# Late values on even steps to the end, masked whole-partition copies of turned P, memory copied before rows, early stores behind the weights, all priority tables re-tuned

## The chip, the cores and the metric

One core of a Trainium2 chip (trn2) runs the whole program; the other cores are idle. The metric is the device time of one launch in microseconds (us), lower is better. The kernel was already tuned: TensorE was busy 97% of the time. Before the change it took a median of 1673.75 us (1672.41 to 1676.7, 4 runs beside the changed kernel). In what follows PE is TensorE (matmuls; PEld its weight loads), DVE is VectorE, ACT is ScalarE, POOL is GpSimd, SP is SyncE; SBUF and PSUM are the two memories in which the program places its tiles; the outputs of the matmuls are in PSUM, in tiles that the program calls banks.

## The reference

Two layers of the same form, each a memory-augmented attention and a dense block with ReLU. The sequence (2048 tokens of width 512) is cut into 64 segments of 32 tokens. In front of each segment stand 8 memory tokens, so a step works on L = 40 tokens with 32 heads of width 128. The memory for the next segment is the first 8 rows of this segment's output: a recurrence over 64 steps.

```python
for s in range(n_seg):                       # 64 segments
    h = concat([mem, x[:, s*32:(s+1)*32]])   # 8 + 32 rows
    q, k, v = h @ Wq, h @ Wk, h @ Wv         # 32 heads x 128
    p = softmax(where(mask, q @ k.T * scale, -1e9))
    o = (p @ v) @ Wo
    mem = o[:, :8]                           # the next step needs this
    outs.append(o[:, 8:])
# x = x + attn(ln(x)); x = x + relu(ln(x) @ w1) @ w2; twice, same weights
```

The kernel runs the two layers interleaved: layer 2 follows 4 steps behind layer 1, so there are 68 steps, and steps 4 to 63 work on 80 columns (40 of each layer). I call these the steady steps. Two of them make a pair, since the dense block and the loading of new rows come once in two steps.

## The kernel before

Every operation is put into a plan with a priority; a small list scheduler in the program then decides which engine runs what and in which order. The priorities come from tuned tables (`PLACE`, `AHEAD`, `RULE`).

```python
def rank(c):     # among the ops that could start now; `stay` favours the tile width now set
    return (c[1].prio - (stay if PE in c[1].cost and c[1].tile in (tile, EITHER) else 0.0), c[1].seq)
```

The stages of a step on PE: Q and K of all heads ("Q/K"), scores, turn of P (a transpose by the identity), attend (PT times V), project (times Wo). The 32 heads of a step go through in five units of 8 or 4 heads. Between the scores and the turn of a unit lies its softmax chain: DVE adds the mask, takes the row maximum and subtracts it, ACT takes the exponentials, DVE takes the sum and its reciprocal, and a product gives P. The result of an attend is copied ("evicted") from PSUM to OT, which the project reads. `COL64` operations use the array in tiles of 64 columns, others in 128; in before's trace a matmul after a change of width starts later. The weights are issued in one fixed order, since each of the DMAs writes the plan's key `"issue"`:

```python
for c, p0, n in (("v",0,1), ("v",1,1), ("v",2,2), ...qk 0, qk 2, o 0, o 2...):
    ...
    plan.op(POOL, 0.75, dma, w=["issue", ("issued", c, p0), ...], lag=1.5)
    plan.op(QUEUE, LOAD * n, land, r=[("issued", c, p0)], w=[("W", c, p0 + i)..., "queue"])
```

After the turn, P is copied from PSUM to SBUF as PT, each of the two heads of a pair into its half of the partitions; the other half stays zero:

```python
for b in range(2):
    def keep(eng, b=b):
        R = slice(64 * b, 64 * b + 64)
        copy_on(eng, PT[R, a_lo:a_hi, 0:2 * nx, b, :], tp[R, A].rearrange(...))
    copy_op(n, keep, r=[tp, PT, "zero PT"], w=[(PT, b)])
```

After the project its bank is read twice: the memory goes to HT, where the next Q/K reads it, and the rows go to OX for the dense block. In the plan the memory copy `ev` and the row copy `rows` are free of each other; in the trace the two reads of the bank follow each other, and here ACT's row copy comes first (DVE's memory copy waits for it for 190.7 us in all, see the page below):

```python
    plan.op(DVE, 0.15, ev, r=[wo], w=[("HTm", i)])          # memory -> HT
    ...
    copy_op(NC4 * SEG * len(aa), rows, r=[wo, "zero ox"], w=[ox])   # rows -> OX
```

"Late values" are V of layer 1's rows for later steps (the row half that does not need the memory). They have much time, so they serve as filling for PE. Groups 5 to 15 are spread over steps near `4 * g - LEAD`, that is until step 43:

```python
for g in range(1, NG):
    plan.mark(*((0, f"g{g}") if g <= EARLY else (4 * g - LEAD - 1, "r")))    # EARLY, LEAD = 4, 8
    prepare_group(g)
```

Of the kernel before, what the change touches and what calls it, by code (L numbers as in the profile page):

```python
# [8 lines left out]
BF = mybir.dt.bfloat16  # L9
# [20 lines left out]
RULE = (0.0474, 165.9433, 849.1155, 931199.0135)  # L30
PERIOD = 35.7447
PLACE = {
    ("attend.mmu0.0", 0): -216.486, ("attend.mmu0.0", 1): 347.606, ("attend.mmu1.0", 0): 191.045,
    ("attend.mmu1.0", 1): -37.14, ("attend.mmu2.0", 0): -46.771, ("attend.mmu2.0", 1): -87.486,
    ("attend.mmu3.0", 0): -34.251, ("attend.mmu3.0", 1): 122.032, ("attend.mmu4.0", 0): 152.031,
    ("attend.mmu4.0", 1): -58.366, ("dense_layer.mm.0", 1): 553.611, ("dense_layer.mm.1", 1): 518.055,
    ("dense_layer.mm.2", 1): 535.954, ("dense_layer.mm.3", 1): 582.949, ("dense_layer.mm.4", 1): 549.423,
    ("dense_layer.mm.5", 1): -563.126, ("finish_pair.turn.0", 1): -571.909, ("g0", 0): 141.998, ("g1", 0): 105.737,
    ("g2", 0): -45.394, ("g3", 0): -40.982, ("g4", 0): 105.238, ("layernorm.turn.0", 1): 118.646,
    ("layernorm.turn.1", 1): 41.01, ("layernorm.turnr.0", 1): -256.199, ("prepare.turns.0", 0): 734.35,  # L40
    ("project.mm.0", 0): 563.031, ("project.mm.0", 1): 33.894, ("project.mm.1", 0): 542.081,
    ("project.mm.1", 1): 183.384, ("project.mm.2", 0): -30.084, ("project.mm.2", 1): 230.376,
    ("project.mm.3", 0): 464.585, ("project.mm.3", 1): 57.605, ("project.mm.4", 0): 4.192,
    ("project.mm.4", 1): -119.585, ("queries_keys.mmu0.0", 0): 15.305, ("queries_keys.mmu0.0", 1): -52.287,
    ("queries_keys.mmu0.1", 0): -466.697, ("queries_keys.mmu0.1", 1): -132.577, ("queries_keys.mmu0.2", 0): 87.033,
    ("queries_keys.mmu0.2", 1): 5.362, ("queries_keys.mmu0.3", 0): -44.757, ("queries_keys.mmu0.3", 1): 81.556,
    ("queries_keys.mmu1.0", 0): 54.963, ("queries_keys.mmu1.0", 1): -50.581, ("queries_keys.mmu1.1", 0): -37.389,
    ("queries_keys.mmu1.1", 1): -11.489, ("queries_keys.mmu1.2", 0): 124.613, ("queries_keys.mmu1.2", 1): 46.342,
    ("queries_keys.mmu1.3", 0): -10.32, ("queries_keys.mmu1.3", 1): -54.319, ("queries_keys.mmu2.0", 0): 131.134,
    ("queries_keys.mmu2.0", 1): 110.056, ("queries_keys.mmu2.1", 0): 188.57, ("queries_keys.mmu2.1", 1): 86.427,  # L50
    ("queries_keys.mmu2.2", 0): 136.518, ("queries_keys.mmu2.2", 1): 105.68, ("queries_keys.mmu2.3", 0): -9.099,
    ("queries_keys.mmu2.3", 1): 98.244, ("queries_keys.mmu3.0", 0): 163.016, ("queries_keys.mmu3.0", 1): 110.95,
    ("queries_keys.mmu3.1", 0): 14.03, ("queries_keys.mmu3.1", 1): 192.637, ("queries_keys.mmu4.0", 0): 339.974,
    ("queries_keys.mmu4.0", 1): 257.046, ("queries_keys.mmu4.1", 0): 340.503, ("queries_keys.mmu4.1", 1): 207.593,
    ("scores.mmu0.0", 0): 149.552, ("scores.mmu0.0", 1): 125.149, ("scores.mmu1.0", 0): 35.849,
    ("scores.mmu1.0", 1): -5.001, ("scores.mmu2.0", 0): 16.784, ("scores.mmu2.0", 1): -51.948,
    ("scores.mmu3.0", 0): 244.506, ("scores.mmu3.0", 1): 56.245, ("scores.mmu4.0", 0): -45.271,
    ("scores.mmu4.0", 1): 447.766, ("scores.turnu0.0", 0): 194.57, ("scores.turnu0.0", 1): 55.105,
    ("scores.turnu1.0", 0): -573.079, ("scores.turnu1.0", 1): 162.901, ("scores.turnu2.0", 0): 146.776,
    ("scores.turnu2.0", 1): -13.477, ("scores.turnu3.0", 0): -142.712, ("scores.turnu3.0", 1): -557.814,  # L60
    ("scores.turnu4.0", 0): -32.301, ("scores.turnu4.0", 1): -558.239, ("values.mm.0", 0): 140.097,
    ("values.mm.0", 1): -46.466, ("values.mm.1", 0): 100.105, ("values.mm.1", 1): 168.241,
    ("values.mm.2", 0): 161.203, ("values.mm.2", 1): 105.472, ("values.mm.3", 0): 200.739,
    ("values.mm.3", 1): -82.814, ("values.mmv0.0", 0): 542.558, ("values.mmv1.0", 1): 574.532,
    ("values.mmv2.0", 0): 480.688, ("values.mmv3.0", 1): 180.687, ("values_narrow.mm.0", 0): 119.158,
    ("values_narrow.mm.0", 1): 313.862, ("values_narrow.mm.1", 0): 19.413, ("values_narrow.mm.1", 1): 340.719,
}
AHEAD = {
    "*late_values.cp": 68.026, "*late_values.put": 167.527, "*layernorm.aggr": -134.458, "*layernorm.eps": -12.177,
    "*layernorm.keep": 157.484, "*layernorm.norm": 235.062, "*layernorm.power": 306.224,  # L70
    "*layernorm.stats": -113.935, "*prepare_group.load": -308.983, "*prepare_group.put": 11.73,
    "*values.ev": 65.226, "attend.ev": -242.579, "dense_layer.relu": -6.21, "dense_layer.relu_last": 178.105,
    "finish_pair.add": -242.042, "finish_pair.add0": -173.051, "finish_pair.add1": -93.035,
    "finish_pair.store": 188.752, "finish_pair.widen": 52.721, "late_values.cp": 212.468, "late_values.put": 18.071,
    "layernorm.aggr": -157.294, "layernorm.eps": 204.671, "layernorm.keep": 168.993, "layernorm.norm": -34.524,
    "layernorm.power": 58.2, "layernorm.stats": 74.815, "load_dense.dma1": 13.513, "load_dense.dma2": 72.207,
    "load_group.get": 70.644, "load_group.load": -212.738, "load_weights.dma": 57.711, "load_weights.hold": 170.204,
    "load_weights.land": -60.531, "make_ident": 215.071, "make_mask": -24.221, "place_values.dma": 32.686,
    "prep_x.cp": -77.977, "prepare.get_memory": -28.532, "prepare.get_x": 90.295, "prepare.keep": 326.132,
    "prepare.place": -93.726, "prepare.zero": 217.012, "prepare.zero_banks": 114.762,  # L80
    "prepare.zero_columns": 19.064, "prepare_group.load": 158.644, "prepare_group.put": 153.519,
    "project.ev": 154.095, "project.first": 306.336, "project.rows": -72.228, "queries_keys.ev": 233.354,
    "scores.block": 179.729, "scores.exp": 6.954, "scores.keep": 236.149, "scores.mul": 385.392,
    "scores.recip": -258.069, "scores.sub": 5.745, "scores.top": -100.433, "scores.total": 132.559,
    "values.ev": 91.194, "values_narrow.ev": -145.426,
}

LOAD = 2.75

EARLY, LEAD = 4, 8  # L90
# [10 lines left out]
def t_dve(n, rate=1):  # L101
    return 0.065 + 1.042e-3 * n / rate

# [51 lines left out]
class Plan:  # L155
# [55 lines left out]
    def order(self):  # L211
# [31 lines left out]
        while left:  # L243
# [32 lines left out]
            for b in o.banks:  # L276
                for i in range(6):
                    if i != e:
                        b.held[i] = max(b.held[i], o.end + LAT[e][i])
# [17 lines left out]
def kernel(  # L297
# [73 lines left out]

    def load_weights():



        for c, p0, n in (("v", 0, 1), ("v", 1, 1), ("v", 2, 2), *((c, p0, 2) for cc, p0 in (("qk", 0), ("qk", 2), ("o", 0), ("o", 2)) for c in cc)):
            def dma(c=c, p0=p0, n=n):
                if c == "o":
                    hs = slice(8 * p0, 8 * (p0 + n))
                    nc.gpsimd.dma_start(out=Wo_sb[:, hs, :], in_=A_Wo.rearrange("h e d -> e h d")[:, hs, :])  # L380
                else:
                    cs = slice(p0 * PW, (p0 + n) * PW)
                    nc.gpsimd.dma_start(out=W_s[c][:, :, cs], in_=W_v[c][:, :, cs])

            plan.op(POOL, 0.75, dma, w=["issue", ("issued", c, p0), *(["issued"] if c == "v" else [])], lag=1.5)

            def land():
                pass

            plan.op(QUEUE, LOAD * n, land, r=[("issued", c, p0)], w=[*[("W", c, p0 + i) for i in range(n)], "queue"])  # L390

        def hold():
            nc.sync.dma_start(out=held[:], in_=Wo_sb[0:1, H - 1, 0:16])

        plan.op(SP, 0.78, hold, r=[("W", "o", 2)], w=["loaded"], lag=0.0)

    def load_dense():
# [3 lines left out]
        def dma2():  # L401
            nc.gpsimd.dma_start(out=w2_sb[:, 0:NFC - 1, :],
                                in_=B_w2[0:(NFC - 1) * 128, :].rearrange("(c p) d -> p c d", p=128))
            nc.gpsimd.dma_start(out=w2_sb[0:F_LAST, NFC - 1, :], in_=B_w2[(NFC - 1) * 128:Dff, :])
# [53 lines left out]
    def prepare():  # L458
# [6 lines left out]
        def zero_banks():  # L465
            for t in b_work.tiles:
                nc.vector.memset(t[:], 0.0)
# [648 lines left out]
```

## Time and profile before

| what | number |
|---|---|
| median time | 1673.75 us |
| span of the profiled run | 1673.3 us, clock 0.995 |
| PE busy | 1621.0 us (97%) |
| end of step 0, of step 3, of step 63, of step 67 | 56.72, 115.77, 1585.81, 1659.12 us |

The step ends are the starts of the last project matmul of that step, from the trace. The page of the kernel before, its first part (busy time, share, count), slices of 1/40 of the span with PE's busy tenths and granted clock, and the chain of waits (shares by line):

```profile
PE 1621.0 (97%) x39689; PEld 1388.0 (83%) x39689; DVE 1049.8 (63%) x3065; ACT 1093.0 (65%) x2759; POOL 127.9 (8%) x337
...
PE   6899999999999999999999999999999999999997
...
PEclk9999999999999999999999999999999999999998
...
PE 84%; DVE 8%; issue 3%; ACT 3%; DMA 2%; POOL 0%; POOLq 0%; DVEq 0%; ACTq 0%
```

So PE bounds the kernel, and what counts is what stands between its matmuls. Busy time does not tell that, because matmuls overlap: one of 80 columns counts as busy for 202 ns, but the next one starts 36 ns after it. I therefore took the starts of neighbouring matmuls from the trace: each form has a median start-to-start time (80 columns 36 ns, 40 columns 25 ns, two 64-wide tiles of 512 columns together 216 ns), whose sum is the work ("floor"); a start after a change of tile width comes later; what is left is waiting.

| before | span | work | width changes | their price | waits |
|---|---|---|---|---|---|
| to the end of step 3 | 115.8 us | 77.3 | 39 | 3.7 | 22.8 (+ 11.9 before the first matmul) |
| steps 4 to 63 | 1470.0 | 1389.9 | 462 | 43.4 | 36.8 |
| steps 64 to 67 | 73.3 | 66.0 | 30 | 2.8 | 4.5 |

At the start the last weight decides. The chain of waits of before, in order of time (start us, us, what):

```profile
16.27 6.02 PE fill L780 x32
...
24.97 29.75 DMA Wo_sb<-in_A_Wo_dram
54.77 2.17 PE st L996 x64
```

The second half of Wo is issued last and lands at 54.8 us. PE is not idle until then, though: Wq and Wk land before it (25.0 to 43.2 us), and the windows of the timeline (start:end, length, busy time with count of PE, PEld, DVE, ACT, POOL, then PE's clock, DMA share, GB/s) show PE busy for 17.7 of the 20 us from 20 to 40. The third line below is a stretch without late values, where PE loses 3% more:

```profile
20.00:40.00 20.00, 17.69 (x310) 10.98 (x308) 6.36 (x21) 10.14 (x23) 5.70 (x16) 1.00 1.03 379
...
300.00:600.00 300.00, 299.14 (x7210) 257.26 (x7210) 193.80 (x548) 206.29 (x509) 22.31 (x62) 1.00 0.11 28
...
1200.00:1500.00 300.00, 291.29 (x7126) 252.94 (x7123) 192.25 (x540) 197.13 (x485) 17.06 (x42) 1.00 0.08 20
```

The copies that the change touches, from the groups of instructions by form (busy us, mean ns; then idle time in front and its releaser). HT, the memory copy, waits for ACT's row copy:

```profile
L721 ACT CAST PT<-work 64x320 bf16<-64x320 f32 x330 | 139.5, 423 | 14.4 <-DVE PT L723 9.6 <-PE work L516 2.7
...
L723 DVE CAST PT<-work 64x160 bf16<-64x160 f32 x188 | 60.3, 321 | 25.6 <-PE work L516 23.5
...
L1012 DVE CAST HT<-st 128x64 bf16<-128x64 f32 x60 | 13.5, 225 | 190.7 <-ACT OX L721 190.7
```

### The profile page before, as it was taken

The page shows a single profiled execution, that of the slowest core. Times are in us where ns is not written, and L with a number is a line of the kernel's source. Part 1 is how long each engine was busy: PE and PEld are TensorE (multiplying, and loading weights), DVE is VectorE, ACT ScalarE, POOL GpSimd, SP SyncE. Part 2 cuts the span into 40 slices and gives each one's busy share as a digit, 9 for nine tenths or more (in the row PEclk, how much of TensorE's full clock was granted, in tenths as well). Part 3 has the DMA queues.
Part 4 walks back from the last instruction along what each step waited for, and adds up shares of the span by engine and source line. Part 5 has one row for each costly group of instructions (what it writes and reads, how often), then busy time and mean ns, then how long its engine had stood idle before and what let it go on. Part 6 is the DMA issues. An engine that isn't in the chain of part 4 may idle for free.

```text
span 1673.3 us, 87959 instructions
## 1 busy us (share of the span) xinstructions
PE 1621.0 (97%) x39689; PEld 1388.0 (83%) x39689; DVE 1049.8 (63%) x3065; ACT 1093.0 (65%) x2759; POOL 127.9 (8%) x337
## 2 busy tenths in 40 slices
PE   6899999999999999999999999999999999999997
PEld 3688888888888888888888888888888888888886
DVE  5466656665665675566667566566656656665664
ACT  3566766766676676666667666666666666666664
POOL 4110000000000010100000000000000000000000
PEclk9999999999999999999999999999999999999998
DMA  9811010111101111000110100000000000000000
GB/s 348 265 45 32 24 29 26 29 32 29 27 24 32 28 30 31 28 24 27 28 29 24 31 25 24 26 26 22 17 25 18 24 20 16 18 19 16 16 6 6
DMA packets 34473, 64.70 MB, mean 39 GB/s; under 512 B 7242, under 2 KB 17874, under 8 KB 34098
## 3 DMA queue, kind: packets, MB, share of 16 engines
q1 hardware_dynamic: 27858, 39.38, 8.4%
q0 software_dynamic: 4624, 18.19, 3.0%
q8 instruction: 311, 5.10, 1.3%
q10 hardware_dynamic: 1616, 1.52, 0.3%
q14 instruction: 64, 0.52, 0.1%
HBM read 33.89 MB, written 12.45 MB: 28 GB/s over the span
## 4 chain that ended last, share of the span: by engine, by line
PE 84%; DVE 8%; issue 3%; ACT 3%; DMA 2%; POOL 0%; POOLq 0%; DVEq 0%; ACTq 0%
PE work L860 32%; PE st L996 18%; PE fill L780 16%; PE fill L516 10%; PE work L969 3%; PE work L889 3%; PE work L516 3%; DMA Wo_sb<-in_A_Wo_dram 2%; DVE P L930 1%; DVE mx L904 1%; DVE es L907 1%; DVE sm L914 1%; DVE es L900 1%; ACT es L911 1%; DVE kT L723 1%
## 5 line engine op out<-in xcount | busy, mean ns | idle before, releaser
L860 PE MATMUL work<-HT,Wk_sb 128*128 128x80 bf16 (+1 forms) x8704 | 357.5, 200 | 1.6 <-issue 1.0
L860 PE MATMUL work<-HT,Wq_sb 128*128 128x80 bf16 (+1 forms) x8704 | 345.6, 199 | 3.9 <-issue 3.9
L996 PE MATMUL st<-OT,Wo_sb 128*128 128x80 bf16 (+1 forms) x8704 | 347.9, 199 | 1.2 <-DMA Wo_sb<-in_A_Wo_dram 0.9
L860 PEld LDWEIGHTS <-Wk_sb 128*128 128x128 bf16 x8704 | 322.3, 99 | 29.0 <-issue 17.2
L996 PEld LDWEIGHTS <-Wo_sb 128*128 128x128 bf16 x8704 | 322.7, 100 | 12.0 <-DMA Wo_sb<-in_A_Wo_dram 1.0
L860 PEld LDWEIGHTS <-Wq_sb 128*128 128x128 bf16 x8704 | 317.4, 99 | 6.3 <-issue 3.9
L721 ACT CAST kT<-work 128x320 bf16<-128x320 f32 (+1 forms) x481 | 197.1, 410 | 130.3 <-PE work L860 98.6
L780 PE MATMUL fill<-Wv_sb,HT 128*64 128x512 bf16 x2048 | 261.3, 382 | 0.0
L900 DVE TENSOR_TENSOR es<-work,maskb 128x320 f32<-128x320 f32 (+2 forms) x340 | 137.1, 405 | 185.9 <-PE work L889 180.0
L721 ACT CAST qT<-work 128x320 bf16<-128x320 f32 (+1 forms) x509 | 208.6, 412 | 57.1 <-PE work L860 16.8
L721 ACT CAST OT<-work 128x320 bf16<-128x320 f32 (+1 forms) x400 | 157.6, 421 | 119.0 <-PE work L969 115.5
L721 ACT CAST vw<-fill 128x512 bf16<-128x512 f32 x263 | 153.7, 585 | 95.0 <-PE fill L780 87.2
L721 ACT CAST PT<-work 64x320 bf16<-64x320 f32 (+2 forms) x454 | 172.8, 382 | 20.6 <-DVE PT L723 9.6
L914 DVE TENSOR_REDUCE sm<-es 128x8 f32<-128x320 f32 (+2 forms) x340 | 134.8, 398 | 41.4 <-ACT es L911 37.7
L911 ACT ACTIVATE es<-es 128x320 f32<-128x320 f32 (+2 forms) x340 | 138.6, 410 | 23.9 <-DVE es L907 22.6
L780 PEld LDWEIGHTS <-HT 128*64 128x64 bf16 x2048 | 97.0, 109 | 64.7
L1012 DVE CAST HT<-st 128x64 bf16<-128x64 f32 (+1 forms) x67 | 14.8, 222 | 207.9 <-ACT OX L721 207.9
L930 DVE TENSOR_TENSOR P<-es,sm 128x320 bf16<-128x320 f32 (+2 forms) x336 | 141.7, 424 | 5.2
L907 DVE TENSOR_TENSOR es<-es,mx 128x320 f32<-128x320 f32 (+2 forms) x340 | 140.6, 416 | 4.6
L904 DVE TENSOR_REDUCE mx<-es 128x8 f32<-128x320 f32 (+2 forms) x340 | 135.2, 400 | 5.6
L889 PEld LDWEIGHTS <-qT 128*40 128x40 bf16 x4096 | 91.5, 98 | 49.5 <-ACT qT L721 3.3
L969 PE MATMUL work<-PT,V 128*128 128x80 bf16 (+1 forms) x1188 | 108.9, 202 | 1.4 <-ACT PT L721 0.5
(89 smaller groups left out, 1761.7 us busy)
## 6 DMA issues: line engine op xcount, KB each, us to landing
V<-vw SPq DMA_DIRECT2D x252, 48.0 KB
V<-vh SPq DMA_DIRECT2D x126, 64.0 KB
vh<-vg SPq DMA_DIRECT2D x22, 256.0 KB
Wq_sb<-in_A_Wq_dram POOLq DMA_DIRECT2D x2, 2048.0 KB, 18.1
Wk_sb<-in_A_Wk_dram POOLq DMA_DIRECT2D x2, 2048.0 KB, 23.0
Wo_sb<-in_A_Wo_dram POOLq DMA_DIRECT2D x2, 2048.0 KB, 27.8
Wv_sb<-in_A_Wv_dram POOLq DMA_DIRECT2D x2, 1024.0 KB, 6.4
Wv_sb<-in_A_Wv_dram POOLq DMA_DIRECT2D x1, 2048.0 KB, 10.8
```

The lines of the kernel that those rows point to most:

```text
L516: nc.tensor.matmul(out_[u:v, :], lhsT=lhsT[:, u:v], rhs=rhs, start=start, stop=stop, tile_position=(0, u))
L721: nc.scalar.copy(out=out_, in_=in_)
L780: nc.tensor.matmul(vp[64 * b:64 * b + 64, :], lhsT=cols[:, c4, :], rhs=Wv_sb[:, c4, n * 512:(n + 1) * 512], start=(c4 == 0), stop=(c4 == N ...
L860: nc.tensor.matmul(qp[:, hi * 2 * L:hi * 2 * L + n], lhsT=W_sb[:, c4, h * Dh:(h + 1) * Dh], rhs=HT[:, c4, c0:c1], start=(c4 == 0), stop=(c ...
L900: nc.vector.tensor_tensor(out=flat(es[:, A]), in0=flat(sp[:, A]), op=ALU.add, in1=maskb[:, a_lo:a_hi, :].unsqueeze(2).to_broadcast([128, n ...
L904: nc.vector.tensor_reduce(out=mx[:, As], in_=es3(), axis=AX.X, op=ALU.max)
L907: nc.vector.tensor_tensor(out=es3(), in0=es3(), op=ALU.subtract, in1=mx[:, As].unsqueeze(2).to_broadcast([128, ns * na, L]))
L911: nc.scalar.activation(out=es[:, A], in_=es[:, A], func=ACTF.Exp, scale=SCALE)
L914: nc.vector.tensor_reduce(out=sm[:, As], in_=es3(), axis=AX.X, op=ALU.add)
L930: (nc.gpsimd if eng == POOL else nc.vector).tensor_tensor(out=o, in0=flat(es[:, A]), op=ALU.mult, in1=sm[:, As].rearrange("p (a s) -> p a ...
L969: nc.tensor.matmul(o[u:u + cols, :, a, :], lhsT=V[:, p, e0 + u:e0 + u + cols], rhs=PT[:, a, 2 * i + h2, :, :], start=True, stop=True, tile ...
L996: nc.tensor.matmul(wo[:, 2 * W * c4 + c0:2 * W * c4 + c1], lhsT=Wo_sb[:, h, c4 * 128:(c4 + 1) * 128], rhs=OT[:, h, c0:c1], start=(h == 0 a ...
```

## The change

Its intent: keep filling for PE up to the end (late values on even steps until step 57), take the memory out of the project's bank before the rows, so that Q/K starts sooner, replace half-partition copies of PT by whole-partition copies with a 0/1 mask as the scale, store the early values behind the weights, and re-tune all tables. The diff, cut to its core (the tables `RULE`, `PERIOD`, `PLACE`, `AHEAD` are new throughout; helpers for buffers, layer norm and zeroing are left out):

```diff
-LOAD = 2.75
-EARLY, LEAD = 4, 8
+LOAD, LOAD_O = 2.55, 2.9
+EARLY, LAST, PACE = 5, 57, 1.3
...
+    def bulk(eng, t, fn, name, size, r=(), w=(), rate=LOAD):
+        plan.op(eng, t, fn, r=r, w=[("issued", *name)], lag=1.5)
+        plan.op(QUEUE, rate * size, land, r=[("issued", *name)], w=[*w, "queue"])
...
-            plan.op(POOL, 0.75, dma, w=["issue", ("issued", c, p0), ...], lag=1.5)
+            bulk(POOL if (c, p0) != ("v", 0) else SP, 0.78, dma, (c, p0), n, w=[...],
+                 rate=LOAD_O if c == "o" else LOAD)
...
             def keep(eng, b=b):
-                R = slice(64 * b, 64 * b + 64)
-                copy_on(eng, PT[R, a_lo:a_hi, 0:2 * nx, b, :], tp[R, A].rearrange(...))
+                o, i = PT[:, a_lo:a_hi, 0:2 * nx, b, :], tp[:, A].rearrange(...)
+                if eng == ACT:
+                    nc.scalar.activation(out=o, in_=i, func=ACTF.Copy, scale=half[:, b:b + 1])
+                else:
+                    nc.vector.tensor_scalar_mul(out=o, in0=i, scalar1=half[:, b:b + 1])
...
-            plan.op(DVE, 0.15, ev, r=[wo], w=[("HTm", i)])
+            plan.op(DVE, 0.15, ev, r=[wo], w=[("HTm", i), ("taken", k)])
...
-            copy_op(NC4 * SEG * len(aa), rows, r=[wo, "zero ox"], w=[ox])
+            copy_op(NC4 * SEG * len(aa), rows, r=[wo, ("taken", k)], w=[ox])
...
+    for i in range(4 * (NG - 1 - EARLY)):          # 40 late values on even steps up to LAST
+        g, p = EARLY + 1 + i // 4, i % 4
+        k = int(LAST - PACE * (4 * (NG - 1 - EARLY) - 1 - i)) // 2 * 2
+        due.setdefault(k, []).append((g, p))
...
+            late_values(g, late[g], [p], [("att", k - 1)])
```

The key `"issue"` is gone, so the scheduler may reorder the weights.

## The prediction

> **What bounds the kernel now.** TensorE's instruction stream. The page's first part has PE busy 1621.0 of 1673.3 us, ACT and DVE at 65% and 63%; the chain that ended last is 84% PE. I priced the stream by start-to-start times of neighbouring matmuls in the trace (80 columns 36 ns, 40 columns 25 ns, 512 columns 216 ns for two 64-wide tiles together). The 39689 matmuls need 1536 us. Besides: 12 us before the first; 532 changes of tile width (128/64/32 columns), 0.115 us extra each, 61 us; other waits 59 us (about 20 before 100 us, 32 from 100 to 1640, 7 at the end); 5 us of tail. [...]
>
> **What the change moves.** By the order of instructions:
> 1. Matmul work is the same (1535 us), but width changes fall from 532 to 366, mostly 4 and 6 per step instead of 7 and 9. 166 x 0.115 = 19 us, all on the critical path. The main gain.
> 2. Late values. Today they run out near step 43; from 1100 us the timeline shows two waits per pair of steps (0.95 us before the P turn, 0.63 us after the project), 1.9 us per pair against 0.25 earlier. After, fill lasts to step 57, so the 0.95 goes: 10 pairs, roughly -10 us.
> 3. Memory ahead of rows. Today ACT copies rows (0.37 us), then DVE the memory (0.225); where little fills it, Q/K starts 0.93 us after the project's last matmul. Memory first makes that 0.24 + 0.225 + 0.055 = 0.52 us. But the new order has no fill between odd-step projects and the next Q/K, so it is paid at every second step: 0.48 x 30 = 15 us, against some 8 today. After even steps 0.65 us of dense matmuls hides it.
> 4. Masked PT copies: same count and elements; consecutive half-partition DVE copies start 0.33 us apart, whole ones 0.23-0.25 (160 elements). Off the path.
> 5. Start. Today the second Wo half lands last, at 54.8 us, 1507 us of matmuls left. After, Wo goes ahead of the second Wq, the first load goes out 1.5 us earlier, 0.5 MB of stores (at about 350 GB/s) move behind the weights: last weight near 52 us (estimate), but 1511 us left. Net about zero.
> 6. Tail unchanged: a serial dense layer, clock granted at half from 1663 us. [...]
>
> **Sum.** 1673 - 1 (work) - 19 (widths) - 3 (waits: -10 + 7) - 1 (start) = about 1649. Range 1636 to 1662.
>
> **What would show it.** Widths: fewer changes at the same price, steady pair of steps 49.2 -> about 48.4 us. Late values: no 0.95 waits after 1100 us. Memory: DVE's HT copy 0.24 us after the project's last matmul (0.64 today); a wait near 0.5 us after odd steps. Start: step 3's project ending near 115 us (116 today).
>
> **What would make it wrong.** Longer one-width runs leave softmax chains less room: in odd steps a P3 turn follows its scores by 2.7 us of PE time (3.05 the shortest today): a few tenths per pair cost 5-10 us. At the start, the last units' Q/K now wait for the last weights with the softmax chain behind[...].

What the trace shows is a median of 0.10 us and a mean of 0.115 us for a change of width as I read it then (0.094 in the later reading of the median), a granted clock of 0.50 from 1663 us to the end, and a wait of 3.85 us in front of a Q/K matmul at 71.59 us, for which the profile shows no releaser.

## The result and the profile after

The changed kernel took a median of 1670.11 us (1669.17 to 1670.9, 4 runs) against 1673.75 us, a ratio of 0.9976 with a 95% interval of 0.9958 to 0.9993: about 4 us faster, within 2%, and outside the predicted range of 1636 to 1662. A ratio here is the mean time of one kernel's fast runs over that of the other's in the same rounds, so it is not quite the ratio of the quoted medians. The profiled span was 1669.2 us at a clock of 0.992.

The page of after, first part, slices and the chain:

```profile
PE 1605.1 (96%) x40146; PEld 1376.4 (82%) x40206; DVE 1098.7 (66%) x3043; ACT 1051.7 (63%) x2662; POOL 160.0 (10%) x387
...
PE   4899999999999999999999999999999999999997
...
PEclk8999999999999999999999999999999999999999
...
PE 82%; DVE 12%; issue 2%; DMA 2%; ACT 1%; ACTq 0%; POOL 0%; POOLq 0%; DVEq 0%
```

PE has 40146 records but PEld 40206: 60 records of the dense block's second matmul (w2) are missing from this trace. For the split of the steady steps I therefore use the run a_issue below, which has all records, the same steady order of matmuls in kind and count, and nearly the same steady span (1461.55 against 1461.34 us).

| | before | after | difference |
|---|---|---|---|
| first matmul | 11.9 us | 7.8 | |
| end of step 3 | 115.77 | 121.61 | +5.8 |
| steps 4 to 63 | 1470.04 | 1461.34 | -8.7 |
| of it width changes, price | 462, 43.4 | 304, 28.9 | -14.5 |
| of it waits | 36.8 | 42.7 | +5.9 |
| steps 64 to 67 | 73.31 | 73.15 | -0.2 |
| after step 67 | 14.14 | 13.08 | -1.1 |
| span | 1673.3 | 1669.2 | -4.1 |

The start got longer although the first matmul came 4 us earlier. The chain of waits of after, its first lines that matter, and then what PE waited for (in total, times, longest):

```profile
8.89 26.30 DMA Wq_sb<-in_A_Wq_dram
...
35.23 1.78 PE work L906 x48
```

```profile
PE work L906 <- DMA Wq_sb<-in_A_Wq_dram: 11.3, 2, 10.5
PE work L906 <- DVE HT L1061: 11.1, 36, 0.3
PE fill L493 <- DMA ob<-in_A_mem_dram: 7.8, 1, 7.8
PE work L532 <- DVE P L976: 5.9, 12, 0.9
```

PE stood still for 10.5 us, until 35.2 us, for the first half of Wq. POOL's timeline shows why: the first half of Wo and the first half of Wk went out in front of it.

```profile
2.35 1.77 POOL L391 DMA_DIRECT2D Wv_sb<-in_A_Wv_dram  x2
4.09 1.18 POOL L388 DMA_DIRECT2D Wo_sb<-in_A_Wo_dram  x1
...
5.83 0.78 POOL L391 DMA_DIRECT2D Wk_sb<-in_A_Wk_dram  x1
...
8.89 0.83 POOL L391 DMA_DIRECT2D Wq_sb<-in_A_Wq_dram  x1
```

The windows of the timeline show PE busy for 9.0 instead of 17.7 us from 20 to 40, with the granted clock at 0.66 of full. The half clock (0.50) was granted from 26.0 to 39.7 us: from 1.3 us after the end of the last matmul, as the profile models it (24.7 us), until 4.5 us after the next one's start. What sets these two moments is not shown. The windows also show that the loss without late values is gone (294.6 of 300 us busy from 1200 to 1500, 291.3 before), while from 300 to 600 PE is busy for less than before (a_issue, which has all records, has 295.9 us there, so most of that is real).

```profile
20.00:40.00 20.00, 9.02 (x134) 5.83 (x132) 4.47 (x11) 4.54 (x10) 2.88 (x7) 0.66 1.03 371
...
300.00:600.00 300.00, 295.09 (x7313) 253.83 (x7322) 206.68 (x548) 194.37 (x478) 27.72 (x67) 1.00 0.10 27
...
1200.00:1500.00 300.00, 294.58 (x7316) 254.44 (x7325) 205.97 (x548) 193.63 (x478) 26.86 (x65) 1.00 0.09 23
```

The copies, from the groups by form. Masked copies take about 0.1 us longer each (530 against 423 ns on ACT), and HT is now released by PE's project and no longer by ACT's OX:

```profile
L999 ACT ACTIVATE PT<-work,half 128x320 bf16<-128x320 f32 x101 | 52.5, 530 | 8.1 <-DVE PT L1001 7.2
...
L1001 DVE TENSOR_SCALAR PT<-work,half 128x320 bf16<-128x320 f32 x259 | 137.0, 539 | 2.2 <-ACT PT L999 0.3
...
L1061 DVE CAST HT<-st 128x64 bf16<-128x64 f32 x60 | 13.5, 225 | 159.6 <-PE st L1045 159.6
```

Where the waits of the steady steps lie, per pair of steps (steps 14 to 61, from the starts of matmuls; the price of 0.094 us of a width change is taken off):

| wait in front of | before | after | a_half | a_short | a_swap | a_pt |
|---|---|---|---|---|---|---|
| Q/K or OX turn, behind an odd project | 0.24 us | 0.48 | 0.48 | 0.48 | 0.89 | 0.48 |
| Q/K, behind the dense block | - | - | - | - | 0.24 | - |
| turn, behind scores | 0.66 | 0.16 | 0.17 | 0.16 | 0.15 | 0.16 |
| turn, behind attend | 0.18 | 0.32 | 0.57 | 0.24 | 0.32 | 0.32 |
| attend, behind the dense block (w1) | - | 0.27 | 0.34 | - | 0.27 | - |
| turn, behind a part of the project | - | 0.05 | 0.15 | - | 0.06 | 0.28 |

A dash is under 0.04 us. So in 30 pairs the waits behind scores fell by some 15 us, those behind the odd project rose by 7, and new waits at attend and turn cost some 14: together the +6 of the table above.

The order of instructions shows what happened to the filling. In before the late values lie one to a step up to step 43. In after all of them lie at the end of odd steps (1 or 2 each), up to step 55, and nothing at all stands between an odd project and the next Q/K.

### The profile page after: what moved, and what is told of

It reads as the page before. It is cut to its first block, busy times and chain, and to the rows that moved or that the text cites. A ratio compares the mean times of both kernels' runs of the same rounds, so it can differ in the third digit from the quotient of the medians.

```text
span 1669.2 us, 88991 instructions
## 1 busy us (share of the span) xinstructions
PE 1605.1 (96%) x40146; PEld 1376.4 (82%) x40206; DVE 1098.7 (66%) x3043; ACT 1051.7 (63%) x2662; POOL 160.0 (10%) x387
## 4 chain that ended last, share of the span: by engine, by line
PE 82%; DVE 12%; issue 2%; DMA 2%; ACT 1%; ACTq 0%; POOL 0%; POOLq 0%; DVEq 0%
PE work L906 34%; PE st L1045 18%; PE fill L826 14%; PE fill L532 7%; PE work L1018 4%; PE work L935 3%; DVE PT L1001 3%; PE work L532 2%; DVE mx L950 2%; DVE es L953 2%; DMA Wq_sb<-in_A_Wq_dram 2%; DVE es L946 1%; DVE sm L960 1%; DVE OT L764 1%; DVE P L976 1%
## 5 line engine op out<-in xcount | busy, mean ns | idle before, releaser
L906 PE MATMUL work<-HT,Wk_sb 128*128 128x80 bf16 (+1 forms) x8704 | 368.6, 199 | 11.8 <-DVE HT L1061 11.1
L906 PE MATMUL work<-HT,Wq_sb 128*128 128x80 bf16 (+1 forms) x8704 | 362.4, 200 | 11.5 <-DMA Wq_sb<-in_A_Wq_dram 11.3
L906 PEld LDWEIGHTS <-Wk_sb 128*128 128x128 bf16 x8704 | 329.8, 99 | 37.9 <-issue 27.2
L906 PEld LDWEIGHTS <-Wq_sb 128*128 128x128 bf16 x8704 | 325.8, 100 | 25.0 <-issue 13.4
L762 ACT CAST kT<-work 128x320 bf16<-128x320 f32 (+1 forms) x539 | 223.3, 414 | 96.2 <-PE work L906 60.3
L762 ACT CAST vw<-fill 128x512 bf16<-128x512 f32 x233 | 136.5, 586 | 147.2 <-PE fill L826 143.1
L1001 DVE TENSOR_SCALAR PT<-work,half 128x320 bf16<-128x320 f32 (+2 forms) x357 | 172.2, 493 | 18.6 <-PE work L532 13.6
L999 ACT ACTIVATE PT<-work,half 128x160 bf16<-128x160 f32 (+2 forms) x323 | 127.3, 430 | 37.3 <-PE work L532 26.6
L728 DVE TENSOR_TENSOR xg<-xg,fill 128x512 f32<-128x512 f32 (+1 forms) x34 | 23.4, 688 | 166.1 <-PE fill L532 161.5
L976 DVE TENSOR_TENSOR P<-es,sm 128x160 bf16<-128x160 f32 (+1 forms) x304 | 121.0, 409 | 4.1
```

The costliest lines, as they stand in the source:

```text
L762: nc.scalar.copy(out=out_, in_=in_)
L906: nc.tensor.matmul(qp[:, hi * 2 * L:hi * 2 * L + n], lhsT=W_sb[:, c4, h * Dh:(h + 1) * Dh], rhs=HT[:, c4, c0:c1], start=(c4 == 0), stop=(c ...
L976: (nc.gpsimd if eng == POOL else nc.vector).tensor_tensor(out=o, in0=flat(es[:, A]), op=ALU.mult, in1=sm[:, As].rearrange("p (a s) -> p a ...
L1001: nc.vector.tensor_scalar_mul(out=o, in0=i, scalar1=half[:, b:b + 1])
```

## The experiments

My theory after the result had three parts. (1) The start lost 10 us because the weights were reordered. (2) In the steady steps the longer one-width runs leave the softmax chains less room, which makes new waits. (3) Memory first and masked copies move these waits. The rival for (2), my first guess, was that the masked copies themselves, each 0.1 us longer, are the new cost. Sixteen kernels ran besides after; all were correct. Every ratio is against before in the same rounds.

| run | what | median us | ratio (95%) |
|---|---|---|---|
| after | | 1670.11 | 0.9976 (0.9958-0.9993) |
| a_issue | after, weights in written order | 1660.43 | 0.9919 (0.9905-0.9932) |
| a_half | after, half-partition PT copies | 1684.03 | 1.0063 (1.0050-1.0075) |
| a_issue_half | both of these | 1673.55 | 1.0002 (0.9989-1.0014) |
| b_tabA | before's code, after's tables | 1718.00 | 1.0267 (1.0253-1.0281) |
| a_tabB | after's code, before's tables | 1689.44 | 1.0103 (1.0088-1.0118) |
| b_mask | before, masked copies | 1667.06 | 0.9969 (0.9954-0.9984) |
| a_short | after, shorter softmax chain | 1658.36 | 0.9916 (0.9901-0.9930) |
| b_short | before, shorter softmax chain | 1666.34 | 0.9964 (0.9947-0.9980) |
| a_rows | after, rows first (other places move too) | 1689.12 | 1.0091 (1.0076-1.0106) |
| b_mem | before, memory first (other places move too) | 1675.96 | 1.0017 (1.0002-1.0032) |
| a_last43 | after, late values end at step 43 | 1672.84 | 0.9998 (0.9983-1.0013) |
| a_issue_short | a_issue with the shorter chain | 1647.83 | 0.9849 (0.9833-0.9866) |
| b_swap | before, memory first, nothing else | 1677.38 | 1.0021 (1.0002-1.0039) |
| a_swap | after, rows first, nothing else | 1691.55 | 1.0100 (1.0083-1.0118) |
| a_pt | after, PT copy ahead of an OT eviction | 1669.97 | 0.9978 (0.9962-0.9995) |
| a_issue_pt | a_issue with that | 1659.57 | 0.9920 (0.9906-0.9935) |

### a_issue, a_half, a_issue_half: the start and the masked copies

The order of the weights is put back with the old key; or the copies of PT are put back to half partitions in the order of after; or both.

```diff
 # a_issue
-        plan.op(eng, t, fn, r=r, w=[("issued", *name)], lag=1.5)
+        plan.op(eng, t, fn, r=r, w=[("issued", *name), *also], lag=1.5)     # also=["issue"] for weights
 # a_half (PT is zeroed once, together with V0)
-                if eng == ACT:
-                    nc.scalar.activation(out=o, in_=i, func=ACTF.Copy, scale=half[:, b:b + 1])
-                else:
-                    nc.vector.tensor_scalar_mul(out=o, in0=i, scalar1=half[:, b:b + 1])
+                R = slice(64 * b, 64 * b + 64)
+                copy_on(eng, PT[R, a_lo:a_hi, 0:2 * nx, b, :], tp[R, A].rearrange(...))
```

> After, with the weight loads put back into the written order (values, then Wq and Wk, Wo last) and nothing else. Theory: the planner put the first half of Wo ahead of Wq and Wk, so Q/K could start only at 35.2 us and PE stood idle for 10.5 us. Then the first Q/K matmul comes near 26 us, the 10.5 us wait is gone, step 3's project ends 5 to 7 us earlier than in the changed kernel (121.6 us there), and the time falls by 5 to 7 us to about 1664. Rival: the start is held by ACT, which issues value copies by DMA for 5 us in front of the first exponentials, or by the last weight whatever it is; then the gain stays below 2 us. The steady steps do not change in either case.

> After, with the PT copies as half-partition plain copies again (PT zeroed once at the start), the PE order of instructions identical. Theory: the masked copy [...] takes 0.11 us longer on ACT and 0.06 on DVE; two of them stand in each chain from turned P to the attend matmul, and the attend waits are what the new order pays. Then the waits in front of and between attend groups (about 0.6 us per pair of steps in the changed kernel) fall by 0.3 to 0.5 us per pair, the time by 9 to 15 us. Rival: the waits come of the order itself, whose one-width runs put the attend too close behind the turn; then the copies' 0.1 us hardly matters and the gain is below 3 us.

> Both edits. If the two causes are separate, their gains add: 14 to 22 us under the changed kernel, near 1652. If the start's delay is absorbed later, or the copies matter only at the start, it is no better than the better of the two alone.

a_issue gained 9.7 us on after, more than expected. Its step 3 ended at 108.86 us (121.61 in after, 115.77 in before), and the stretch from 20 to 40 us is nearly as full as in before, at full clock:

```profile
20.00:40.00 20.00, 16.68 (x262) 10.85 (x263) 6.71 (x18) 10.36 (x23) 5.50 (x9) 1.00 1.04 371
```

The steady steps stayed (1461.55 us). The last weight lands at 53.9 us in a_issue and at 51.6 in after, so the faster start has the later last weight. So the start is settled: the reordered weights cost after some 10 us.

a_half went the other way from both readings: it is 14 us slower than after, not faster. My guess that masked copies are a cost fell with it, and so did the prediction's "off the path". What PE waited for in a_half:

```profile
PE work L532 <- DVE P L976: 14.3, 42, 0.9
PE work L906 <- DVE HT L1058: 11.1, 36, 0.3
...
PE work L1015 <- DVE PT L764: 4.7, 28, 0.2
```

Waits for P rose from 5.9 to 14.3 us although P's own operations are the same. The reason is in the neighbours of the copies. I took, over the steady steps, the time from the start of one operation to that of the next on the same engine, less the first one's duration, for neighbours without a wait between them (medians; negative means overlap). Before and b_mask (below) have the same order on every engine and differ only in the form of the copies; which half a copy of before writes follows from the plan:

| | before, lower half | before, upper half | b_mask, masked |
|---|---|---|---|
| DVE, something then PT | -0.084 us | +0.032 | -0.084 |
| DVE, PT then something | -0.076 | +0.031 | -0.084 |
| ACT, something then PT | -0.105 | +0.024 | -0.112 |
| ACT, PT then something | -0.103 | +0.024 | -0.121 |

A copy into the lower half or over all partitions overlaps both its neighbours; in before a copy into the upper half never does (some 300 such neighbours, all with a gap). That is 0.11 us lost at either side on DVE and 0.13 on ACT, some 0.22 to 0.26 us a copy, where half of the copies go to the upper half; a_half shows the same +0.031 for them on DVE. What counts on DVE is the change of half, not the upper half itself: in a_half, where DVE copies into the upper half follow each other (29 times), they overlap by 0.080 us. For ACT this is not shown. The masked copies are longer, by 0.05 us on DVE (539 against 485 ns for 320 elements in after and a_half) and by 0.107 us on ACT (530 against 423). Taken together, a pair of masked copies of 320 elements holds its engine for less time than a pair of half copies, by an estimate of some 0.06 us on ACT (with the 547 ns of b_mask; 0.09 with the 530 of after) and 0.13 us on DVE (durations and overlaps added up). Why a change of half costs the overlap is not shown. Nor is how much of the 107 ns is the mask's: the plain copy ran as another instruction (CAST, not ACTIVATE) and wrote half as many partitions.

a_issue_half gained and lost as the sum (1673.55): the two effects are independent.

### b_mask: the masked copies alone

The same edit of `keep` in before's code, with before's tables and an identical order on PE.

> The kernel before with one part of the change alone: the copies of turned P run over whole partitions with a 0/1 mask as the scale. The order of every engine's instructions stays as it was (PE checked: identical). In the order of after, taking the mask away cost 14 us. If masked copies help wherever turns and attends wait for them, because a whole-partition copy overlaps its neighbours while a half-partition one waits for them, this runs 4 to 10 us faster than before: 1663 to 1669, with the 128x320 ACT copy still near 530 ns. Rival: in the order of before there is more room behind the turns, and the copies are off the path: 1671 to 1678, no difference.

The overlap meant here is that of the table above (on DVE -0.084 us for masked copies); of the half copies only those into the upper half lack it (+0.032 us, against -0.084 for the lower).

It gained 5 us on before, in the expected range; the steady steps went from 1470.0 to 1463.1 us, their waits from 36.8 to 30.0. ACT's copies took 547 ns and still helped. Masked copies are worth 5 us in the old order and 14 in the new one.

### b_tabA, a_tabB: code and tables apart

> Before's code with after's tables of priorities alone. Its order of instructions has 411 width changes (532 before, 366 after), pairs of steps with 10, plain half copies, rows copied ahead of memory, and no matmuls between an odd step's project and the next Q/K. Theory: the fewer changes come of the tables (-11 us), but without memory first each odd step waits about 0.9 us for Q/K instead of 0.5 (30 x 0.9 = 27 us); with today's fill gone the time is 1670 to 1685. Rival: memory first has nothing to do with it and the tables alone give the gain: below 1665.

> The code of after with the priority tables of before: 527 width changes, weights issued in the written order at the start. The fourth corner of code x tables (before's code: 1673 with its own tables, 1718 with after's). If code and tables help independently this would be faster than after by some 45 us, which nobody expects. If the tables only fit the code that they were tuned with, it is slower than both: 1680 to 1700. Rival: the gain of the change lies in the code (masked copies, late values to step 57), and the old tables serve it nearly as well: 1655 to 1672.

Before's code under after's tables took 1718.0 us, far outside both ranges; its steady steps had 344 width changes and 82 us of waits. After's code under before's tables took 1689.4 us, in the first theory's range: step 3 ended at 125.7 us, and there were 454 changes in the steady steps. So neither part does the work alone: by themselves the tables cost 45 us and the code 17, together they gain 4. The weights went out in written order in a_tabB, so it is the lost key together with the new tables that reordered them.

### a_short, b_short: the room of the softmax chains

The row maximum and its subtraction emit nothing. The plan still counts them, so every engine's order stays. The result is still right here because these scores are small; no run tests larger ones.

```diff
         def top():
-            nc.vector.tensor_reduce(out=mx[:, As], in_=es3(), axis=AX.X, op=ALU.max)
+            pass
         def sub():
-            nc.vector.tensor_tensor(out=es3(), in0=es3(), op=ALU.subtract, in1=mx...)
+            pass
```

> The kernel after with the softmax chain shortened: the row maximum and its subtraction emit nothing (the result is the same here, since the scores are small), everything else and the order of all engines stays. Each chain loses two DVE operations of about 0.4 us. The steady steps of after have 42 us of waits, 15 of them between an odd project and the next Q/K. If the waits at turn and attend come from too little room for the chains behind the longer one-width runs, they go: 20 to 27 us faster than after, 1643 to 1650. Rival: these waits come from the copies' queue behind the turn and not from the chain's length: 1660 to 1668.

> The same cut made in the kernel before: no row maximum, no subtraction, same order of all engines (PE checked: identical). Its waits in the steady steps are 37 us, with more of them between project, OX turn and Q/K (which the chain does not touch). Theory of the chain's room: 8 to 16 us faster than before, 1657 to 1665, so that with short chains after leads by 10 to 18 us, near the predicted price of the width changes. Rival: both gain alike, and the lead stays at 3 to 5 us.

a_short gained 11 us on after (waits of the steady steps 42.7 to 31.3), less than the 20 to 27 of the theory and more than the rival's 2 to 10; b_short gained 6 on before, just short of its range. The lead of after over before went from 4 to 8 us, between the ranges of the two theories. In the steady steps alone, a_short is 13.1 us ahead of b_short (1450.19 against 1463.32), close to the 14.5 us of the width changes. So the width changes do pay what they are worth once the chains have room; about 11 us of the 27 that I put down to the chains go with them. The cut does two things at once, though: it shortens every chain, and it takes two operations off DVE, which may let other work through sooner. The 0.48 us behind the odd project did not move at all, as they should not.

### a_last43: where the late values end

```diff
-EARLY, LAST, PACE = 5, 57, 1.3
+EARLY, LAST, PACE = 5, 43, 0.95
```

> The kernel after with the late values finished by step 43 as in before, instead of step 57 (same work, 366 width changes). In after's own trace four steps without late values (60 to 64) have about 0.9 us more waits than four with them, against 3.1 us more in before. If after's order really needs the late values less, this costs 2 to 5 us: 1672 to 1675. If each pair without late values costs the 0.95 us that the prediction read from before, 7 pairs make it 6 to 8 us slower: 1676 to 1678.

It took 1672.84 us, some 2.7 us more than after: in the first range, not in the second. Late values to the end are worth less in the new order than the prediction read from the old one, where the waits of four steps went from 1.3 to 4.5 us when the late values ran out.

The trace goes further: the 2.7 us are not the price of late values that end early. Step 3 ended at 124.7 us (121.6 in after), and the steady steps took 1459.3 us, 2.0 less than after's (1.1 of it work that moved in front of them). The loss lies in step 2: there DVE stood still for 5.6 us until the rows of a group had been loaded, the memory copy was behind that operation in DVE's queue, and PE waited 4.8 us for HT. So in the steady steps of the new order late values after step 43 gain nothing: with them the waits are smaller by some 0.5 us per pair after step 44 and larger by some 0.2 us per pair before.

### b_mem, a_rows, b_swap, a_swap: memory first

b_mem adds the key `("taken", k)` to before, a_rows reverses it in after. Both shift other instructions. b_swap and a_swap change only which of the two reads of the bank is emitted first after the plan has been made; the order on PE, ACT, POOL and SP is identical (a_swap: 7 places differ on DVE).

```diff
 # b_swap, after planning (a_swap: the other way round)
+            late = [o for o in out if o.kind == "project.rows" and o.step == k]
+            for o in [o for o in out if o.kind == "project.ev" and o.step == k]:
+                if late and out.index(o) > min(map(out.index, late)):
+                    out.remove(o); out.insert(min(map(out.index, late)), o)
```

> The kernel before with memory first alone. In its first 43 steps late values or dense matmuls lie between nearly every project and the next Q/K and hide the copy; after that they are gone, and some 10 odd boundaries would gain 0.4 us each: 3 to 6 us faster than before, 1667 to 1670. Rival: no gain, since the OX turn, which then has to wait longer for its rows, stands in that place: 1671 to 1676.

> The kernel after with one part undone: the rows are copied out of the project's bank before the memory again (matmuls, width changes 366, start and masked copies as in after; the order of equal units inside a step shifts a little). If the memory copy is the end of every odd boundary, as the wait of 0.48 us there says, it comes about 0.4 us later at each of 30 odd steps, while dense matmuls hide it after even steps: 10 to 16 us slower than after, 1680 to 1686. Rival: other waits behind it shrink by as much and nothing changes: 1668 to 1673.

> The kernel before with memory first alone and nothing else moved: the order on every engine is identical, only the row copy now waits for the memory copy instead of the other way round. Where fill hides the copy (to step 43) nothing changes; in the ten pairs after it the wait behind the odd project is 0.63 us, with the OX turn in it. If the memory copy is the end of that wait: 3 to 6 us faster than before, and b_mem's loss came from its reordering. If the OX turn is the end, which is now 0.22 us later, or 0.2 us later in all 30 pairs: no gain or up to 7 us slower, as b_mem.

> The kernel after with rows first and nothing else moved (the order of PE, ACT, POOL and SP is identical, 7 places differ on DVE). If the odd boundaries pay exactly the later memory copy: the wait there goes from 0.48 to about 0.88 us, 11 to 13 us slower than after, 1681 to 1684, and the other 6 us of a_rows were its reordering. If the later Q/K also makes the chains behind it late: 17 to 20 us slower, as a_rows.

The two mixed runs first: b_mem lost 2 us on before (its rival) and a_rows 19 on after (more than either theory had). The clean ones gave much the same totals: b_swap lost 4 us, a_swap 21 (just above its second range). So the reordering is not needed to explain the losses. The traces of the mixed runs show that their totals are made up differently: in a_rows the steady steps lost 13.7 us (20.1 in a_swap) and the start 3.5; in b_mem the first four steps ended 7.3 us later, 2.8 of it work that moved there, and the steady steps were 3.3 us shorter, their waits unchanged. The clean runs are the ones to go by. The timeline of an odd boundary in after, and then in a_swap (start us, us, engine, line, operation; in brackets the idle time in front and what ended it):

```profile
706.98 0.22 DVE L1061 CAST HT<-st 128x64 bf16<-128x64 f32 x1 [1.86 <-PE st L1045]
707.24 0.37 ACT L762 CAST OX<-st 128x256 bf16<-128x256 f32 x1 [1.08 <-DVE HT L1061]
707.26 1.31 PE L906 MATMUL work<-HT,Wk_sb 128*128 128x80 bf16 x32 [0.31 <-DVE HT L1061]
```

```profile
713.95 0.37 ACT L769 CAST OX<-st 128x256 bf16<-128x256 f32 x1 [0.82 <-PE st L1052]
714.35 0.23 DVE L1068 CAST HT<-st 128x64 bf16<-128x64 f32 x1 [2.26 <-ACT OX L769]
714.63 1.06 PE L913 MATMUL work<-HT,Wk_sb 128*128 128x80 bf16 x25 [0.72 <-DVE HT L1068]
```

The last project matmul of these steps started at 706.74 and 713.71: Q/K follows 0.52 us later in after and 0.92 in a_swap. The odd boundary went from 0.48 to 0.89 us as expected (12 us in 30 pairs), and the even one, where the dense block's 0.65 us no longer hide the copy, got 0.24 us (7 us in 30 pairs). PE's waits for HT in a_swap:

```profile
PE work L913 <- DVE HT L1068: 24.5, 36, 0.7
```

In before it is the other way. There the OX turn stands in front of Q/K and needs the rows: in b_swap PE's waits for OX rose from 5.8 to 9.6 us (the first line is before's):

```profile
PE fill L516 <- ACT OX L721: 5.8, 13, 0.5
PE fill L523 <- ACT OX L728: 9.6, 15, 0.7
```

The steady steps of b_swap took 1.9 us more. Its first four steps ended 4 us later (119.7); why is not shown: only 0.7 us of waits for OX lie there, and the profiled run (1681.34 us) was the slowest of its four. So memory first is worth about 20 us in the new order and nothing in the old one.

### a_pt, a_issue_pt: DVE's queue or the chain

The timeline of after (DVE and PE of step 20) shows the wait of 0.27 us in front of the attend. The turn is issued at 526.43 and ACT has copied its half by 527.6; DVE's copy stands behind two subtractions of later units and an eviction of OT:

```profile
526.69 1.14 DVE L953 TENSOR_TENSOR es<-es,mx 128x320 f32<-128x320 f32 x2
...
527.04 0.54 ACT L999 ACTIVATE PT<-work,half 128x320 bf16<-128x320 f32 x1
...
527.75 0.48 DVE L764 CAST OT<-work 128x320 bf16<-128x320 f32 x1
528.15 0.54 DVE L1001 TENSOR_SCALAR PT<-work,half 128x320 bf16<-128x320 f32 x1
...
528.74 0.23 PE L1018 MATMUL work<-PT,V 128*64 128x80 bf16 x2 [0.21 <-DVE PT L1001]
```

a_pt exchanges the last two DVE operations shown, in every even step, after planning:

```diff
+        for a, b in zip(line, line[1:]):          # neighbours on DVE
+            if a.kind == "attend.ev" and b.kind == "scores.keep" and a.step % 2 == 0:
+                out.remove(b); out.insert(out.index(a), b)
```

> The kernel after; in every even step one pair of neighbours on DVE is exchanged, the copy of turned P now before the eviction of an attend (OT) that stood ahead of it. Nothing else moves: PE, ACT, POOL and SP in identical order, no operation shorter. If the attend waits for DVE's queue, its copy comes about 0.5 us earlier and the wait of 0.27 us per pair between the dense matmuls and the attend goes: 6 to 9 us faster than after, 1660 to 1664. If it waits for the length of the softmax chain, nothing changes: 1668 to 1672. If the eviction of OT that now comes later delays the project, it is slower.

> The same exchange with the weights issued in the written order: the gains of a_issue (10 us) and of the exchange (6 to 9 us) add: 1652 to 1655. If the queue is not the cause: as a_issue, 1659 to 1661.

The exchange did what it should: the copy comes at once after the subtractions, and the attend has no wait.

```profile
525.99 1.13 DVE L959 TENSOR_TENSOR es<-es,mx 128x320 f32<-128x320 f32 x2
...
526.86 0.70 ACT L963 ACTIVATE es<-es 128x320 f32<-128x320 f32 x2
527.05 0.54 DVE L1007 TENSOR_SCALAR PT<-work,half 128x320 bf16<-128x320 f32 x1
...
527.51 0.48 DVE L770 CAST OT<-work 128x320 bf16<-128x320 f32 x1
527.75 0.20 PE L1024 MATMUL work<-PT,V 128*64 128x80 bf16 x2
...
527.91 0.69 DVE L966 TENSOR_REDUCE sm<-es 128x8 f32<-128x320 f32 x2
```

And nothing came of it: 1669.97 us against 1670.11, and 1659.57 against 1660.43 with the start repaired. In the table of waits the 0.27 us in front of the attend have gone, and the wait of the next turn, behind the first part of the project, has grown from 0.05 to 0.28. That turn needs the P of a later unit, at the end of its softmax chain, which has hardly moved. The attend's wait was in series with the chain's, so removing it alone is worth nothing. a_short removed both. So the place of this one copy in DVE's queue is not what counts; the end of the chain is.

What holds the end of the chain stays open. It can be the chain's own length, or the copies that stand in DVE's queue between the chain's operations. The exchange left both copies in front of the sum, and the lines above show the queue at work: the two exponentials end at 527.56, but DVE is busy with the eviction of OT and takes the sums from 527.91 on. A sum that finds DVE free starts 0.03 us after its exponentials; the 29 sums behind this eviction in a_pt start 0.54 us after (medians). No run moved the eviction behind the sums, and a_short, which takes work off DVE as well, does not part the two.

### What came out fastest

a_issue (1660.43 us) and a_issue_pt (1659.57) beat both kernels and are the same within their intervals. a_issue_short took 1647.83 us:

> Both cuts that helped together: weights issued in the written order, and softmax chains without the row maximum and its subtraction. If the start and the steady steps are independent the gains add (10 and 11 us): 1647 to 1651. Rival: with the start repaired the chains have other waits in front of them, and only part of it remains: 1653 to 1660.

The gains added as expected, and in the trace each is where it was alone: step 3 ends at 108.4 us (108.9 in a_issue), the steady steps take 1451.0 us (1450.2 in a_short). It is the fastest, but it leaves out the row maximum, so it is a measure of what the chains cost and no general replacement.

## Why the prediction was wrong

The prediction was 1649 (1636 to 1662); the time was 1670.11. Point by point, with the prediction's terms:

- **What bounds the kernel: right.** PE's stream and what stands between its matmuls; every experiment moved the time through waits of PE.
- **Step 1, width changes, -19: right in mechanism, too large in size.** The changes fell from 532 to 366 as read. The mean of 0.115 us contained waits; the price is 0.094 in the median, nearly the same in both traces, so 166 changes are 15.6 us (14.5 in the steady steps).
- **Step 2, late values, -10: the waits named did shrink, but not because of the late values, and the gain did not stay.** The turns behind scores gained even more, 0.66 to 0.16 us per pair, some 15 us in 30 pairs. a_last43 gives the late values after step 43 nothing in the steady steps of the new order, so the size of this term came near by luck; which part of the new order shortened these waits is not shown.
- **Step 3, memory first, +7 net: right.** HT's copy starts 0.24 us after the start of the project's last matmul, Q/K 0.52, both as written; the boundary rose from 0.24 to 0.48 us per pair, 7 us. a_swap shows what it is worth: without memory first the new order would lose some 20 us more.
- **Step 4, masked copies "off the path": wrong.** They gain 14 us in the new order (a_half) and 5 in the old (b_mask). The prediction had read the overlap from the trace (starts 0.23 to 0.25 us apart instead of 0.33) and did not ask which waits of PE end with these copies.
- **Step 5, start, "net about zero": this step failed.** I compared only the last weight's landing (52 against 54.8 us, which was right) with the work left. I had seen that Wo goes ahead of the second Wq and did not ask what PE would have to do from 25 us on if the first Wq came late. It had nothing: 10.5 us idle, and a granted clock of 0.50 from 26.0 to 39.7 us. Step 3's project ended at 121.6 us, not 115. a_issue puts 9.7 us on this one thing, although its last weight lands 2.3 us later than after's.
- **Step 6, tail unchanged: right** (1 us shorter).
- **The sum of waits, "-10 + 7": this step failed too.** Measured, it is -15 + 7 + 14 = +6. The +14 are new waits at attend and turn. "What would make it wrong" named the cause (longer one-width runs leave the softmax chains less room) at 5 to 10 us, but the sum held nothing for it. a_short removes 11 us of them; a_pt shows that the end of the chain holds them and not the place of one copy. Whether it is the chain's length or DVE's load in front of it stays open.

So of the some 20 us by which the estimate of 1649 fell short, about 7 are the start (+5.8 for -1), 9 the waits (+6 for -3) and 4 the width changes (-15.6 for -19). These are differences of terms, not separate measurements.

The larger lesson is in the tables. Before's code with after's order loses 45 us, after's code with before's order 17. The new order saves 14.5 us of width changes and uses up room that hid the copies; masked copies (14 us) and memory first (20 us) make up for that. The parts of such a change can't be priced one by one from the old trace: in the old order memory first is worth nothing, because there the rows are the ones waited for.

## What to carry to other kernels

When a change lets a scheduler reorder loads, ask for each load what the bound engine can still do before it lands, not only when the last one lands. When a fill or an ordering is taken from one place to another, list every dependent chain that the old place was hiding and book it in the sum, not among the risks. And a wait that vanishes under an edit is a gain only if the next wait in the same chain does not grow by as much: look for where it went before you keep the edit.
